# Attention scores as three fp16 passes instead of one fp32 pass, with a mask, a low half and weight pieces put elsewhere

## The chip, the core and the metric

One NeuronCore of a Trainium2 chip runs the program. It has a matrix engine (TensorE, PE in the profile; its weight loads are listed as PEld), VectorE (DVE), ScalarE (ACT), GpSimd (POOL) and SyncE (SP), which issues most DMAs. Each engine works through its own queue in the order in which the program was written, and waits in place when what it needs isn't there. The metric is the device time of one execution in microseconds; the time of a kernel is the median of its runs.

## What is computed

Keys and values of 8 batches, 8 heads and 576 rows are averaged over 8 rows each, so that 72 pooled keys remain. The attention over them gives 4608 rows of 512, and each row then goes through one of 8 experts (a matrix of 512x1024, a ReLU, a matrix of 1024x512), chosen by the largest of 8 logits, and is scaled by the softmax of that logit.

```python
k_p = k.reshape(B, H, Sp, pool, D).mean(axis=3)
v_p = v.reshape(B, H, Sp, pool, D).mean(axis=3)
scores = scale * np.matmul(q, k_p.transpose(0, 1, 3, 2))
attn = np.exp(scores - np.max(scores, axis=-1, keepdims=True))
attn = attn / (np.sum(attn, axis=-1, keepdims=True) + 1e-09)
out = np.matmul(attn, v_p)
...
h = np.maximum(x_sorted[lo:hi] @ w1[e], 0.0)
y_sorted[lo:hi] = h @ w2[e]
```

## The kernel before

The program has two parts. The attention takes the first 190 us, in 36 **units** (a unit is 128 query rows of one batch with all 8 heads; every ninth unit takes 64 rows of each of two batches). The experts take the rest, in blocks of 256 rows, and were left alone.

The order is written by hand: the loop at line 975 emits unit after unit, and `put(i, position, f)` hangs a step on a position of unit i (`q`, `pe`, `act`, `dve`, `pe2`, `sp`, `act2`, `dve2`), which `run(i, position)` emits there. What concerns the change, in the order of one unit i:

- `u_pt` (line 487) turns unit i's probabilities P with five transposes into the PSUM tile `pp`, which has one buffer, and ScalarE copies them to `pt` (line 496). In seven units one more matmul puts the mask `mk` beside them in `pp` (line 494).
- `g_s` (line 452) makes the scores of two heads (a half stage A here, a half stage Z at the unit's end), by one fp32 matmul a head. Such a matmul serves two units: on its 128 partitions stand the 64 features of a query row of one unit and the 64 of a row of the other, and the keys stand twice in `BD` (three tiles, one a batch), in the upper 64 partitions for the first 72 columns and in the lower 64 for the other 72, with zeros beside them. So 144 columns come out. The turned queries stand in `qT`.
- `g_qt` (line 432) turns four heads of a later group of queries into a PSUM tile `pq`, and ScalarE copies it to `qT` (line 445).
- `k_pe`, `v_pe` and `u_pe` each come once a batch, in units of their own: they turn the pooled keys, turn the pooled values, and multiply the values by the router's matrix. Each writes a `pq` tile. `k_act` and `v_act` (lines 362, 379) copy the keys from it into the first half of `BD`; for batches 2 to 7 a DMA collected in `moves` (line 1012) then copies them into the second half.
- `g_min` (line 477) takes the smallest score on VectorE, `g_exp` (line 484) the exponentials on ScalarE.
- `masked` (line 410) writes the masked values V into `VB`, on VectorE, from the mask in `pp`.
- `u_pv` (line 498) multiplies `pt` by V into `po`, which has one buffer; `u_nrm` (line 531) divides by the sums on VectorE (lines 544, 546, 548) and so frees `po`. Between its steps `fill()` emits steps of the router of an earlier group (lines 588 to 658).

All of `g_qt`, `k_pe`, `v_pe`, `u_pe` and the router share the tile name `pq` with **two buffers, used in turn**: whoever comes next takes the buffer used the time before last, and must wait until its readers are done. `wsplit` (line 104) splits an expert's weights into fp16 halves; its pieces `h` and `s` are ScalarE work over 128x1024 each, at `act` and `act2` of units 12 to 31 in the table at line 832.

## Time and profile before

| | |
|---|---|
| median of 3 runs | 605.59 us (604.68 to 605.96) |
| the profiled execution | 608.13 us, span of its instructions 606.2 us |
| busy share of the span | PE 96%, PEld 72%, DVE 44%, ACT 47%, POOL 45% |
| granted TensorE clock, mean | 0.99 |

The span is counted from the first instruction; all positions in the trace are microseconds from there. A busy matmul is counted from its issue to its modelled end, so two that overlap fill the row without a gap; the PEld rows show better when TensorE takes up the next piece of work. In brackets stands how long an engine sat idle ahead of an instruction, and what released it.

### The profile page before, as it was taken

The page shows a single profiled execution, that of the slowest core. Times are in us where ns is not written, and L with a number is a line of the kernel's source. Part 1 is how long each engine was busy: PE and PEld are TensorE (multiplying, and loading weights), DVE is VectorE, ACT ScalarE, POOL GpSimd, SP SyncE. Part 2 cuts the span into 40 slices and gives each one's busy share as a digit, 9 for nine tenths or more (in the row PEclk, how much of TensorE's full clock was granted, in tenths as well). Part 3 has the DMA queues.
Part 4 walks back from the last instruction along what each step waited for, and adds up shares of the span by engine and source line. Part 5 has one row for each costly group of instructions (what it writes and reads, how often), then busy time and mean ns, then how long its engine had stood idle before and what let it go on. Part 6 is the DMA issues. An engine that isn't in the chain of part 4 may idle for free.

```text
span 606.2 us, 15226 instructions
## 1 busy us (share of the span) xinstructions
PE 581.4 (96%) x4473; PEld 436.6 (72%) x4474; DVE 268.2 (44%) x545; ACT 285.0 (47%) x633; POOL 270.7 (45%) x527
## 2 busy tenths in 40 slices
PE   7899999999998989989999999999999999999995
PEld 7788999999894747747676765767756677567663
DVE  6545655675664264025752873323623471133022
ACT  2766688889931262226642762233522452222122
POOL 5798899997966424220432332122411242211212
PEclk9999999999999999998999999999999999999999
DMA  8999899784594549942987689143332224421200
GB/s 250 302 313 242 293 319 283 266 278 155 142 312 166 175 120 326 341 101 63 311 260 222 181 263 341 61 108 82 79 91 52 83 62 108 108 49 39 69 17 32
DMA packets 96271, 107.10 MB, mean 177 GB/s; under 512 B 54446, under 2 KB 64686, under 8 KB 96240
## 3 DMA queue, kind: packets, MB, share of 16 engines
q1 hardware_dynamic: 89520, 85.42, 49.6%
q0 software_dynamic: 6720, 21.28, 9.3%
q8 instruction: 17, 0.28, 0.2%
q14 instruction: 14, 0.11, 0.1%
HBM read 72.99 MB, written 23.37 MB: 159 GB/s over the span
## 4 chain that ended last, share of the span: by engine, by line
PE 51%; PEld 4%; issue 3%; ACT 1%; PEldq 0%; POOLq 0%; ACTq 0%; DVE 0%; POOL 0%; DVEq 0%
PE po L1042 14%; PE pq L1042 11%; PE ps L964 6%; PE pp L964 3%; PE pq L964 3%; PE ps L955 2%; PE ps L956 2%; PE ps L957 2%; PEld L964 1%; PEld L1042 1%; PE pp L957 1%; PE pq L956 1%; PE pq L957 1%; PE pp L955 1%; PE pq L955 1%
## 5 line engine op out<-in xcount | busy, mean ns | idle before, releaser
L1042 PEld LDWEIGHTS <-bd 128*128 128x128 f16 x936 | 91.3, 98 | 110.1 <-issue 3.1
L1203 POOL TENSOR_TENSOR spacer<-ql,iG 1x1 f32<-1x1 f32 x44 | 20.8, 472 | 199.2 <-ACT ql L1199 191.8
L1036 DVE SCALAR_TENSOR_TENSOR bd<-ps,bd 128x512 f16<-128x512 f32 (+1 forms) x44 | 27.6, 630 | 182.8 <-ACT bd L1033 180.0
L484 ACT ACTIVATE both<-ps,nmx 128x72 f32<-128x72 f32 x288 | 68.9, 349 | 3.1 <-DVE nmx L477 3.1
L1033 ACT ACTIVATE bd<-ps 128x512 f16<-128x512 f32 (+1 forms) x44 | 24.1, 549 | 96.4 <-PE L964 76.3
L513 PE MATMUL po<-vb,pt 128*128 128x146 f32 (+5 forms) x480 | 66.8, 301 | 1.2 <-ACT pt L496 1.2
L513 PEld LDWEIGHTS po<-vb,pt 128*128 128x128 f32 (+1 forms) x480 | 62.1, 178 | 4.4 <-ACT pt L496 2.5
L1042 PE MATMUL po<-w,bd 128*128 128x512 f16 x264 | 59.3, 379 | 1.0 <-issue 1.0
L1042 PE MATMUL po<-kv,bd 128*128 128x512 f16 x264 | 58.8, 379 | 0.0
L964 PEld LDWEIGHTS <-qt 128*128 128x128 f16 x528 | 48.6, 99 | 11.8 <-issue 4.7
L1204 POOL DMA_INDIRECT out_dram<-ql,iG x44 | 46.2, 1051 | 21.0 <-issue 19.9
L964 PEld LDWEIGHTS <-w 128*128 128x128 f16 x480 | 42.1, 100 | 10.8 <-ACT kv L114 2.8
L1042 PE MATMUL pq<-kv,bd 128*128 128x512 f16 x216 | 48.1, 379 | 0.0
L467 PE MATMUL ps<-bd,qT 128*128 128x144 f32 x256 | 44.4, 297 | 2.5 <-DVE bd L739 0.8
L1042 PE MATMUL pq<-w,bd 128*128 128x512 f16 x192 | 44.7, 389 | 1.6 <-ACT bd L1033 1.6
L1199 ACT ACTIVATE ql<-po,gB 128x512 f32<-128x512 f32 x22 | 15.0, 683 | 57.7 <-PE L964 36.2
L663 POOL DMA_INDIRECT x_by_expert<-both,rpos x36 | 35.5, 987 | 13.1 <-issue 5.6
L467 PEld LDWEIGHTS ps<-bd,qT 128*128 128x128 f32 x256 | 34.9, 190 | 3.6 <-DVE bd L739 0.9
L477 DVE TENSOR_REDUCE nmx<-ps 128x4 f32<-128x288 f32 x72 | 32.0, 452 | 11.1 <-PE ps L467 10.3
L496 ACT ACTIVATE pt<-pp 128x640 f32<-128x640 f32 x36 | 25.5, 709 | 23.3 <-PE pp L491 14.3
L964 PE MATMUL ps<-kv,qt 128*128 128x256 f16 (+1 forms) x264 | 32.8, 266 | 3.6 <-issue 2.7
L864 DVE TENSOR_TENSOR bd<-vb,bd 128x1024 f16<-128x1024 f32 x22 | 27.0, 1225 | 19.1 <-ACT bd L861 9.2
(243 smaller groups left out, 1194.8 us busy)
## 6 DMA issues: line engine op xcount, KB each, us to landing
both<-in_moe_w_dram SPq DMA_DIRECT2D x6, 2048.0 KB, 12.2
st<-in_moe_w_dram SPq DMA_DIRECT2D x6, 2048.0 KB, 13.7
vb<-x_by_expert SPq DMA_DIRECT2D x16, 578.0 KB
st<-in_moe_w_dram SPq DMA_DIRECT2D x8, 1024.0 KB
kv<-in_k_dram SPq DMA_DIRECT2D x6, 1024.0 KB
kv<-in_v_dram SPq DMA_DIRECT2D x6, 1024.0 KB
qt<-in_q_dram SPq DMA_DIRECT2D x6, 1024.0 KB
kv<-in_k_dram SPq DMA_DIRECT2D x4, 512.0 KB
```

The costliest lines, as they stand in the source:

```text
L467: nc.tensor.matmul(ps[:, x * 2 * KP:(x + 1) * 2 * KP], t[:, h, :], BD[b % 3][:, :, h, :], start=True, stop=True)
L477: nc.vector.tensor_reduce(nmx, ps[:, 0:4 * KP].rearrange("p (h x) -> p h x", x=KP), axis=AX.X, op=OP.min)
L484: nc.scalar.activation(p[:, h * KP:(h + 1) * KP], ps[:, x * KP:(x + 1) * KP], AF.Exp, bias=nmx[:, x:x + 1], scale=-1.0)
L496: nc.scalar.activation(pt, pp[:, 0:640], AF.Copy)
L513: nc.tensor.matmul(po[m, half, cols], pt[:, c * 128 + m.start:c * 128 + m.stop], VB[(b + s) % 3][:, c, sl, 0:CW], start=first.get(half, Tr ...
L663: st = nc.gpsimd.indirect_dma_start(out=xs, out_offset=bass.IndirectOffsetOnAxis(ap=Z["pos"][:, u:u + 1], axis=0), in_=X[:, u, :], in_offs ...
L864: nc.vector.tensor_tensor(col(xh[:, :, 1]), row(xg), col(xh[:, :, 0]), op=OP.subtract)
L955: nc.tensor.matmul(dst, wh, xT[:, d, 0:n], start=(d == 0), stop=False)
L964: nc.tensor.matmul(dst, W1[s][z][:, d, c], xT[:, x, 0:n], start=(z == 0 and x == 0), stop=(z == 1 and d == DC - 1))
L1036: V.scalar_tensor_tensor(pair(hT[1], k, n), ups_of(k, n), 0.0, pair(hT[0], k, n), op0=OP.max, op1=OP.subtract)
L1042: nc.tensor.matmul(y, hT[x][:, f, 128 * j:128 * j + 128], W2[s][z][:, f, :], start=(half == x == z == f == 0), stop=(half == z == 1 and f ...
L1204: st = nc.gpsimd.indirect_dma_start(out=out, out_offset=bass.IndirectOffsetOnAxis(ap=iG[:, j:j + 1], axis=0), in_=ys[j], in_offset=None, b ...
```

## The change

The scores no longer use fp32 operands. Queries and keys are each held as a high fp16 number and a low fp16 number (the rest), and `g_s` adds three passes, high by high, low by high and high by low, in one accumulation. The queries are scaled by 2^-3 and the keys by its inverse. `BD` and `qT` become fp16 tiles with one more index for high and low; they keep their size.

The high halves are written by the ScalarE copies that were there. The low halves are new VectorE instructions that read the same PSUM tile `pq` again: `q_low`, of 128x512, behind `g_min(A)` of the unit; and `k_low`, of 64x512 for the keys that `k_pe` turned and 64x64 for those that `v_pe` did, collected in `klows` and emitted by `k_lows` at the unit's end, behind `act2` and `dve2`. The copy into the second half of `BD` (`moves`) goes out there too, for both halves of the number in one DMA, and no longer ahead of `g_s(Z)`. At the start batch 0 gets the same: its second half moves from VectorE (line 739) to ScalarE, and two `k_low` and a `q_low` follow on VectorE.

Two further steps move. `masked` has a position of its own, `mask`, ahead of `g_min(A)`. The `h` and `s` pieces of the weights move mostly from the end of a unit to the new position `pt` of the next, straight behind ScalarE's copy of the turned P.

```diff
-    BD = [loads.tile([128, 2, H, KP], F32, name=f"bd{i}") for i in range(3)]
+    BD = [loads.tile([128, 2, 2, H, KP], F16, name=f"bd{i}") for i in range(3)]
...
-    SC = 1.0 / (POOL * math.sqrt(D))
+    SC = 1.0 / (POOL * math.sqrt(D) * SQ)
...
+    def k_low(b, s, src, lo, hi):
+        nc.vector.scalar_tensor_tensor(half(b, s, 1)[:, lo:hi], src, -SC, half(b, s, 0)[:, lo:hi], op0=OP.mult,
+                                       op1=OP.subtract)
+
+    klows = []
+
+    def k_lows():
+        while klows:
+            k_low(*klows.pop(0))
+        while moves:
+            nc.sync.dma_start(*moves.pop(0))
...
-            nc.scalar.activation(half(b, s)[:, 0:512], pm[64 * s:64 * s + 64, :], AF.Copy, scale=-SC)
+            nc.scalar.activation(half(b, s, 0)[:, 0:512], pm[64 * s:64 * s + 64, :], AF.Copy, scale=-SC)
+            klows.append((b, s, pm[64 * s:64 * s + 64, :], 0, 512))
...
-            moves.append((half(b, 1), half(b, 0)))
+            moves.append((BD[b % 3][64:128, :, 1], BD[b % 3][0:64, :, 0]))
...
-            QT[G] = work.tile([128, 8, 128], F32, name="qT", bufs=2)
+            QT[G] = work.tile([128, 2, 8, 128], F16, name="qT", bufs=2)
...
-            nc.scalar.activation(QT[G][:, 4 * j:4 * j + 4, :].rearrange("p h t -> p (h t)"), pq, AF.Copy)
+            nc.scalar.activation(qh, pq, AF.Copy, scale=SQ)
+            return lambda: nc.vector.scalar_tensor_tensor(qw, pq, SQ, qh, op0=OP.mult, op1=OP.subtract)
...
+    PASS = ((0, 0), (1, 0), (0, 1))
...
-                nc.tensor.matmul(ps[:, x * 2 * KP:(x + 1) * 2 * KP], t[:, h, :],
-                                 BD[b % 3][:, :, h, :], start=True, stop=True)
+                for y, z in PASS:
+                    nc.tensor.matmul(ps[:, x * 2 * KP:(x + 1) * 2 * KP], t[:, y, h, :], BD[b % 3][:, z, :, h, :],
+                                     start=(y, z) == PASS[0], stop=(y, z) == PASS[-1])
...
-    nc.vector.tensor_scalar(half(0, 1), pm[64:128, 0:H * KP], -SC, None, op0=OP.mult)
+    nc.scalar.activation(half(0, 1, 0), pm[64:128, 0:H * KP], AF.Copy, scale=-SC)
+    q_low()
+    for s in range(2):
+        k_low(0, s, pm[64 * s:64 * s + 64, 0:H * KP], 0, H * KP)
...
-        put(at, "dve", masked, b)
+        put(at, "mask", masked, b)
...
-    for j, h, x, p in ((0, (12, "act2"), (13, "act2"), 15), (1, (14, "act2"), (17, "act2"), 24),
+    for j, h, x, p in ((0, (13, "pt"), (14, "pt"), 15), (1, (15, "pt"), (18, "pt"), 24),
...
         run(i, "pe")
+        run(i, "mask")
         if A:
             g_min(*A)
+        for f in lows:
+            f()
+        if A:
             fill()
...
-        while moves:
-            nc.sync.dma_start(*moves.pop(0))
         if Z:
             g_s(*Z)
         u_nrm(i, (lambda: g_min(*Z)) if Z else None)
         run(i, "act2")
         run(i, "dve2")
+        k_lows()
```

Three places show what stands in a row. The first is VectorE in unit 24, which turns the keys of batch 7 and also begins the router of units 18 to 23 (L588 to L612 before, L609 to L633 in the change). Before, from the two minima (L477) to the next two:

```order
L477 TENSOR_REDUCE nmx<-ps 128x4 x2
L588 TENSOR_REDUCE pq<-both 128x48
L590 TENSOR_REDUCE rm<-pq 128x6
L594 TENSOR_TENSOR ra<-pq,rm 128x48
L595 TENSOR_TENSOR pq<-pq,rm 128x48
L544 TENSOR_SCALAR ri<-po 128x8
L601 TENSOR_TENSOR pq<-pq,down 128x48
L602 TENSOR_REDUCE rm_1976<-pq 128x6
L546 RECIPROCAL ri<-ri 128x8
L612 TENSOR_TENSOR roh<-pq,rm_1976 128x48
L548 TENSOR_TENSOR both<-po,ri 128x576
```

In the change the same stretch begins so (L462 is `q_low`):

```order
L498 TENSOR_REDUCE nmx<-ps 128x4 x2
L462 SCALAR_TENSOR_TENSOR qT<-pq,qT 128x512
L609 TENSOR_REDUCE pq<-both 128x48
L611 TENSOR_REDUCE rm<-pq 128x6
L615 TENSOR_TENSOR ra<-pq,rm 128x48
```

and ends so (L352 is `k_low`, L569 the last step of `u_nrm`):

```order
L622 TENSOR_TENSOR pq<-pq,down 128x48
L623 TENSOR_REDUCE rm_2269<-pq 128x6
L567 RECIPROCAL ri<-ri 128x8
L633 TENSOR_TENSOR roh<-pq,rm_2269 128x48
L569 TENSOR_TENSOR both<-po,ri 128x576
L498 TENSOR_REDUCE nmx<-ps 128x4
L352 SCALAR_TENSOR_TENSOR bd_155<-pq,bd_155 64x512
```

`q_low` now stands ahead of the router's steps and of `u_nrm`, and `k_low` behind `u_nrm` and the minimum of Z.

The second place is TensorE in unit 25, from the scores of A to the turned values, before (with what an instruction waits for in brackets; L440 turns the queries, L368 the values):

```order
L467 MATMUL ps_1996<-bd0_154,qT_1887 128x144 [waits DVE_49,Activation_49]
L467 MATMUL ps_1996<-bd0_154,qT_1887 128x144
L440 MATMUL pq_2003<-ident_67,qt0_150 128x128 [waits Activation_49]
L440 MATMUL pq_2003<-ident_67,qt0_150 128x128 x3
L368 MATMUL pq_2010<-ident_67,vp_1800 128x128 [waits DVE_49,Pool_49]
```

and in the change (L488, L455 and L382 are the same steps):

```order
L488 MATMUL ps_2290<-bd0_154,qT_2162 128x144
L488 LDWEIGHTS qT_2162
L488 MATMUL ps_2290<-bd0_154,qT_2162 128x144
L455 MATMUL pq_2301<-ident_67,qt0_150 128x128 [waits DVE_49,PE_49]
L455 MATMUL pq_2301<-ident_67,qt0_150 128x128 x3
L382 MATMUL pq_2308<-ident_67,vp_2057 128x128 [waits DVE_49,PE_49,Pool_49]
```

The turn of the queries takes the buffer that `k_pe` of unit 24 used. It waited for ScalarE's copy of the keys, and now waits for VectorE, whose last reading of that buffer is `k_low`.

The third place is ScalarE around unit 24 (L496 and L517 copy the turned P, L445 and L461 the queries, L118 and L119 are an `s` piece). Before:

```order
L118 ACTIVATE st_64<-st_64 128x1024
L496 ACTIVATE pt<-pp 128x640
L445 ACTIVATE qT<-pq 128x512
L484 ACTIVATE both<-ps,nmx 128x72 x8
L362 ACTIVATE bd_155<-pq 64x512
L598 ACTIVATE rex<-ra 128x48
```

and in the change:

```order
L517 ACTIVATE pt<-pp 128x640
L119 ACTIVATE st_64<-st_64 128x1024
L461 ACTIVATE qT<-pq 128x512
L505 ACTIVATE both<-ps,nmx 128x72 x8
L375 ACTIVATE bd_155<-pq 64x512
L619 ACTIVATE rex<-ra 128x48
```

The piece has gone from ahead of the copy of P to between it and the copy of the queries.

## Rows read from the trace of the kernel before

**Rows 1.** Busy time by stretch: start:end, length, engines, granted clock, DMA share, GB/s.

```profile
33.00:139.00 106.00, 105.54 (x877) 100.20 (x878) 61.74 (x179) 85.04 (x283) 97.70 (x105) 1.00 0.90 281
139.00:169.00 30.00, 28.81 (x244) 26.94 (x243) 17.74 (x55) 27.69 (x81) 25.12 (x41) 1.00 0.57 169
190.00:204.00 14.00, 11.20 (x51) 4.85 (x51) 4.91 (x31) 2.46 (x4) 3.92 (x11) 0.88 0.30 98
```

**Rows 2.** Timeline of weight loads, units 24 and 25: start, length, engine, line, count.

```profile
133.48 0.55 PEld L467 LDWEIGHTS ps<-bd,qT 128*128 128x128 f32 x4
133.96 0.59 PEld L491 LDWEIGHTS pp<-ident,both 128*128 128x128 f32 x5
...
135.00 0.48 PEld L440 LDWEIGHTS pq<-ident,qt 128*128 128x128 f32 x4
...
136.15 1.76 PEld L513 LDWEIGHTS po<-vb,pt 128*128 128x128 f32 x12
...
139.57 0.48 PEld L440 LDWEIGHTS pq<-ident,qt 128*128 128x128 f32 x4
```

**Rows 3.** Timeline of TensorE: fp16 matmuls of 128 (L722) and 256 columns.

```profile
11.18 0.61 PE L722 MATMUL po<-ones 128*128 128x128 f16 x8
...
168.49 0.27 PE L955 MATMUL ps<-kv,w 128*128 128x256 f16 x1
...
168.70 0.27 PE L957 MATMUL ps<-kv,w 128*128 128x256 f16 x1
```

**Rows 4.** Groups by line and shape: busy us, mean ns of one, idle before.

```profile
L1036 DVE SCALAR_TENSOR_TENSOR bd<-ps,bd 128x512 f16<-128x512 f32 x34 | 23.4, 691 | 135.0 <-ACT bd L1033 132.1 <-issue 2.8
...
L118 ACT ACTIVATE st<-st 128x1024 f32<-128x1024 f32 x8 | 9.0, 1126 | 0.0
```

**Rows 5.** Timeline of VectorE, units 24 and 25.

```profile
132.29 0.86 DVE L588 TENSOR_REDUCE pq<-both 128x48 f32<-128x384 f32 x1 [0.54 <-ACT qT L445]
...
134.44 0.75 DVE L548 TENSOR_TENSOR both<-po,ri 128x576 f32<-128x576 f32 x1
135.10 0.81 DVE L477 TENSOR_REDUCE nmx<-ps 128x4 f32<-128x288 f32 x2
...
139.58 0.20 DVE L635 TENSOR_TENSOR rt<-pq,roh 128x48 f32<-128x48 f32 x1
```

**Rows 6.** Timeline of ScalarE, unit 24.

```profile
130.74 0.71 ACT L496 ACTIVATE pt<-pp 128x640 f32<-128x640 f32 x1 [0.31 <-PE pp L491]
131.66 0.60 ACT L445 ACTIVATE qT<-pq 128x512 f32<-128x512 f32 x1 [0.22 <-PE pq L440]
```

**Rows 7.** Timeline of VectorE and weight loads, units 6 and 7.

```profile
57.66 0.91 DVE L477 TENSOR_REDUCE nmx<-ps 128x4 f32<-128x288 f32 x2
...
57.78 0.49 PEld L440 LDWEIGHTS pq<-ident,qt 128*128 128x128 f32 x4
```

**Rows 8.** The same two engines, units 15 and 16.

```profile
96.40 0.92 DVE L477 TENSOR_REDUCE nmx<-ps 128x4 f32<-128x288 f32 x2
...
96.99 0.25 PEld L368 LDWEIGHTS pq<-ident,vp 128*128 128x128 f32 x2
```

**Rows 9.** The same two engines, units 19 and 20.

```profile
113.64 0.20 DVE L635 TENSOR_TENSOR rt<-pq,roh 128x48 f32<-128x48 f32 x1
...
113.80 0.48 PEld L440 LDWEIGHTS pq<-ident,qt 128*128 128x128 f32 x4
```

**Rows 10.** The same two engines, unit 18 and the start of unit 19's `u_pv`.

```profile
106.67 0.87 DVE L588 TENSOR_REDUCE pq<-both 128x48 f32<-128x384 f32 x1 [1.11 <-ACT qT L445]
...
110.15 1.77 PEld L513 LDWEIGHTS po<-vb,pt 128*128 128x128 f32 x12
```

**Rows 11.** Timeline of VectorE, GpSimd and weight loads, start of the program.

```profile
11.74 0.76 DVE L739 TENSOR_SCALAR bd<-pp 64x576 f32<-64x576 f32 x1 [1.86 <-ACT bd L738]
...
18.42 0.19 POOL L773 TENSOR_TENSOR spacer<-vp 1x1 f32<-1x1 f32 x1 [9.33 <-DVE vp L335]
...
32.21 0.11 PEld L370 LDWEIGHTS pq<-ident,vp 128*64 128x64 f32 x1 [1.31 <-POOL vp L314]
```

More of the change, by code (lines that the diff above doesn't have):

```diff
@@ L25 @@
 UPAT = (33, 34, 35)
+SQ = 2.0 ** -3
 HS = (0, 1, 3, 5, 5)
@@ L345, in pool_v, with half @@
         pool(kv[(2 * b + 1) % 3], KVS["vp", b], (part,))
-    def half(b, s):
-        return BD[b % 3][64 * s:64 * s + 64, s].rearrange("p h x -> p (h x)")
+    def half(b, s, y):
+        return BD[b % 3][64 * s:64 * s + 64, y, s].rearrange("p h x -> p (h x)")
+    def k_low(b, s, src, lo, hi):
[7 more added lines that the diff above has]
+            nc.sync.dma_start(*moves.pop(0))
     def k_pe(b):
@@ L378, in v_act @@
         for s in range(min(b, 2) and 3 - min(b, 2)):
-            nc.scalar.activation(half(b, s)[:, 512:576], pm[64 * s:64 * s + 64, 384:448], AF.Copy, scale=-SC)
+            nc.scalar.activation(half(b, s, 0)[:, 512:576], pm[64 * s:64 * s + 64, 384:448], AF.Copy, scale=-SC)
+            klows.append((b, s, pm[64 * s:64 * s + 64, 384:448], 512, 576))
         if b > 1:
-            moves.append((half(b, 1), half(b, 0)))
+            moves.append((BD[b % 3][64:128, :, 1], BD[b % 3][0:64, :, 0]))
         vT = KVS["vT", b] = work.tile([128, 384], F32, name="vT", bufs=1)
@@ L441, in g_qt @@
         if j == 0:
-            QT[G] = work.tile([128, 8, 128], F32, name="qT", bufs=2)
+            QT[G] = work.tile([128, 2, 8, 128], F16, name="qT", bufs=2)
+        qh, qw = (QT[G][:, y, 4 * j:4 * j + 4, :].rearrange("p h t -> p (h t)") for y in range(2))
         def put_q():
-            nc.scalar.activation(QT[G][:, 4 * j:4 * j + 4, :].rearrange("p h t -> p (h t)"), pq, AF.Copy)
+            nc.scalar.activation(qh, pq, AF.Copy, scale=SQ)
+            return lambda: nc.vector.scalar_tensor_tensor(qw, pq, SQ, qh, op0=OP.mult, op1=OP.subtract)
         return put_q if hold else put_q()
@@ L458, in g_s @@
                 for s in range(2):
-                    bd = BD[(b + s) % 3].rearrange("p s h x -> p (s h) x")
-                    rhs = bd[:, 2 * x:2 * x + H + 2:H + 1, :]
-                    nc.tensor.matmul(ps[64 * s:64 * s + 64, (x % 2) * 2 * KP:(x % 2 + 1) * 2 * KP],
-                                     t[:, x, 64 * s:64 * s + 64], rhs, start=True, stop=True)
+                    for y, z in PASS:
+                        rhs = BD[(b + s) % 3][:, z].rearrange("p s h x -> p (s h) x")[:, 2 * x:2 * x + H + 2:H + 1, :]
+                        nc.tensor.matmul(ps[64 * s:64 * s + 64, (x % 2) * 2 * KP:(x % 2 + 1) * 2 * KP],
+                                         t[:, y, x, 64 * s:64 * s + 64], rhs, start=(y, z) == PASS[0],
+                                         stop=(y, z) == PASS[-1])
             slots = [(4 * j + x, 0) for x in range(4)]
@@ L466, in g_s @@
             for x, h in enumerate(hs):
-                nc.tensor.matmul(ps[:, x * 2 * KP:(x + 1) * 2 * KP], t[:, h, :],
-                                 BD[b % 3][:, :, h, :], start=True, stop=True)
+                for y, z in PASS:
+                    nc.tensor.matmul(ps[:, x * 2 * KP:(x + 1) * 2 * KP], t[:, y, h, :], BD[b % 3][:, z, :, h, :],
+                                     start=(y, z) == PASS[0], stop=(y, z) == PASS[-1])
             slots = [(h, s) for h in hs for s in range(2)]
@@ L735 @@
     turned((4, 2, 3))
-    g_qt(0, 0)
+    q_low = g_qt(0, 0)
     turned((0, 1))
-    nc.scalar.activation(half(0, 0), pm[0:64, 0:H * KP], AF.Copy, scale=-SC)
-    nc.vector.tensor_scalar(half(0, 1), pm[64:128, 0:H * KP], -SC, None, op0=OP.mult)
-    g_qt(0, 1)
+    nc.scalar.activation(half(0, 0, 0), pm[0:64, 0:H * KP], AF.Copy, scale=-SC)
+    nc.scalar.activation(half(0, 1, 0), pm[64:128, 0:H * KP], AF.Copy, scale=-SC)
+    q_low()
+    for s in range(2):
+        k_low(0, s, pm[64 * s:64 * s + 64, 0:H * KP], 0, H * KP)
+    q_low = g_qt(0, 1)
     nc.tensor.matmul(warm[:, 0, 384:399], ident, mk.rearrange("p c s -> p (c s)"), start=True, stop=True)
@@ L746 @@
     g_min(0, 1)
+    q_low()
     g_exp(0, 1)
@@ L755 @@
     keep_warm(8)
-    turned_q()
+    turned_q()()
     u_pt(0)
@@ L760 @@
     v_act(0)
-    g_qt(1, 1)
+    q_low = g_qt(1, 1)
     now(1, 0)
@@ L767 @@
     g_min(1, 1)
+    q_low()
     load_qh(1, 0)
@@ L981 @@
             u_pt(i)
+        run(i, "pt")
+        lows = []
         if i == 0:
-            g_qt(*turns.pop(i))
+            lows.append(g_qt(*turns.pop(i)))
         if A:
@@ L989 @@
         if i in turns:
-            g_qt(*turns[i])
+            lows.append(g_qt(*turns[i]))
         if Y and keyed:
```

2 lines of the change are left out of this document (1 added, 1 removed), and 6 rows, old and new, of the table n.

## The prediction

> **What bounds the kernel now.** I read first the busy time by stretch [rows 1], because the change touches only the attention, and its share has three phases. Between 33 and 139 us TensorE is busy 105.5 of 106 us with its clock at 1.00; VectorE has 44 us to spare there and ScalarE 21. Between 139 and 169 us ScalarE is the fullest beside TensorE, 27.7 of 30 us. So what shortens TensorE's rows before 139 us shortens the program, unless TensorE is made to wait; after it that is no longer sure.
>
> The timeline of weight loads then gives the price of each piece, since one piece begins where the last ends [rows 2]: a half stage of scores is two fp32 matmuls, and from its first load to that of the next piece pass 133.96 - 133.48 = 0.48 us. In this stretch TensorE goes from piece to piece with hardly an idle bracket. That is the thing to look for: the order of before has just enough distance between a piece and what it waits for, and a new wait on a `pq` buffer costs its whole length.
>
> **The passes.** The trace of before has no 144-column fp16 matmul. Its nearest are 256 columns, each with a weight load of its own, which start 0.105 us apart (168.49 to 168.70 for two), and 128 columns: eight in 0.61 us, and since a single one of 256 shows 0.27 - 0.105 = 0.165 us of tail, (0.61 - 0.165)/8 = 0.056 us apart [rows 3]. On the line between these, 144 columns make 0.062 us. Six of them make 0.375 us in place of 0.48: **0.105 us saved** for a half stage. By the ends 0.056 and 0.105 us it would be +0.14 saved or 0.15 lost. I take 0.062, because 144 lies next to 128. Units 2 to 26 with one batch hold 44 such half stages in the stretch that TensorE bounds: 44 x 0.105 = **-4.6 us** (ends -6.4 and +6.6). The half stages of units with two batches are 64 rows each and I count nothing for them; the 14 after 139 us lie under ScalarE.
>
> The Trainium skill ("TensorE: Matmul & The Clock Gate", section "Back-to-back issue gap") says that a stream of weight load and matmul pairs holds about 81 ns a matmul at 128 columns, where 56 ns is the gap of a lone one. The eight of [rows 3], which load weights each, speak against it at 56 ns. By the page six passes would be an estimated 0.5 us, and the saving gone. It is the third rival below.
>
> **The low halves on VectorE.** Nothing like them stands in the attention of before, but the experts have the same operation, out of PSUM with an fp16 operand, 128x512 in 0.69 us [rows 4]; I take 0.65 to 0.69 for `q_low` and for the 64x512 `k_low` (fewer partitions don't shorten an instruction: 64x576 took 0.76 us [rows 11]). At 256 columns the same line would be cheaper, so the lower bound is half, 0.35 us; the upper is the 0.76 of the start. Some 26 `q_low` in the stretch are 18 us of VectorE's 44 spare ones. Throughput is therefore no issue; what matters is who stands behind them, and when the buffer comes free.
>
> **Unit 24 to 25, the worst place.** In the change `g_qt` of unit 25 waits for `k_low` of unit 24, which stands behind `q_low`, the router's start, `u_nrm` and two minima. P's copy starts at 130.74 and `qT` at 131.66 [rows 6]. An `s` piece of 1.05 us (its row, 1.13, is modelled with overlap [rows 4]) is now between them: `qT` comes at 132.4 and is done at 133.0. `q_low` takes VectorE to 133.65, where the router started at 132.29 [rows 5]: 1.36 later. From there VectorE is a chain without a gap, so the minima of Z go from 135.10 to 136.46; the later of the two ends 0.4 after that for the first and `k_low` runs from about 136.86 to 137.55. TensorE wants `g_qt` at 135.00 [rows 2], less three saved half stages, 134.7. Hold: **2.85 us**. Half as long a low step would leave 2.2.
>
> **The other units with `k_low`.** The same reading at the other four, always from the last instruction of VectorE and the load that wants the buffer: unit 6 to 7, minima at 57.66 begin 0.55 later for `q_low` and `k_low` ends at 59.3, wanted at 57.78 less three half stages: 1.8 [rows 7]. Unit 15 to 16, without a router's start: the first minimum at 96.40 ends and `k_low` runs to about 97.4, for a `pq` wanted at 96.7: 0.7 [rows 8]; it stands ahead of the values' turn at 96.99. Unit 19 to 20: behind a router step at 113.64, `k_low` to 114.5 for 113.80 less three: 0.8 [rows 9]. Unit 10 to 11 is like 15 to 16 with less before it: 0.55. Sum with unit 24: **+6.7 us**. Where `v_pe`'s buffer has a 64x64 `k_low` (short, but again behind `u_nrm` and the minima) I get 0.7 at units 7 to 8 and 25 to 26 and 0.25 at 11 to 12 and 20 to 21: **+1.9 us**. All of them are bounded below by nought (if VectorE is ahead, nobody waits) and above by one and a half times.
>
> **Routers without keys.** In unit 18 the router begins at 106.67, behind `qT` [rows 10]; a weight piece ahead of the copy makes `qT` 1.0 later, `q_low` adds 0.65, and the last of `u_nrm`, which frees `po`, ends at 111.25 instead of 109.6 (where the minima of Z begin). `u_pv` wanted it at 110.15 [rows 10], less two half stages, 109.9: 1.4. In unit 12 it is 0.5 in the same way. **+1.9 us.**
>
> **The start.** VectorE copied the second half of batch 0's keys in 0.76 us at 11.74 [rows 11]; that copy goes to ScalarE, ahead of the first scores either way, and `q_low` and two `k_low` (some 2 us) come on VectorE, ahead of the pooling of V that GpSimd waits for (row at 18.42). Values' turns later wait 1.31 us for GpSimd (row at 32.21) [rows 11], so this delay reaches TensorE. Part of it lies in waits that are there: **+1.0 us**, from 0 to 2.
>
> **Costed at nothing.** The mask of V moves ahead of `g_min(A)`: 1.1 us of VectorE in seven units, which delays the minima and the exponentials by as much, but ScalarE has 21 us spare in the stretch and the turned P of the next unit is not the last to come; without that cover up to 1 us each. The `moves` go out some 2 us later on SP; what they copy is needed three units on, and behind them on SP's queue stand loads that are as far from their use. The weight pieces move by half a unit, in both directions, and ScalarE's total over 139 to 169 us stays at 27.7 of 30 [rows 1]: 0, between -0.7 and +1.5.
>
> **Sum.** -4.6 + 6.7 + 1.9 + 1.9 + 1.0 = +6.9 us. The profiled execution took 608.13 us, 2.5 over the median of the runs (605.59) and spread over all of it, so by itself it would become 615.0; against the median, **612.5 us**.
>
> **Rivals.** First, the holds don't bite: VectorE gets to `k_low` before TensorE comes, because TensorE itself has been slowed by something else or the short form of the low step is cheap. For it: VectorE is idle 42% of the stretch. Against it: in unit 24 its rows stand end to end. The passes' saving and half of the start's delay remain, 605.59 - 4.6 + 0.5 = 601.5 us. Second, half of the holds: 605.59 - 4.6 + 1.0 + 5.25 = 607.2, or 606.4 with the low step at half its length in the K units; I take 606.4, no change. Third, the passes save nothing (the skill's rule, above): 612.5 + 4.6 = 617.1. The eight at 56 ns speak against it; for it only that they share one operand and these don't. Fourth, the hold at unit 25 lets the clock fall from 2.4 to 1.2 GHz for a time. In 190 to 204 us, where TensorE stands idle for 2.8 of 14 us, it was granted 0.88 on the mean of the two levels [rows 1]; a hold of 2.85 us that costs a like share of the 14 us after it is 0.12 x 14 = 1.7 us, 614.2. The rival that ends on the other side is the first; it decides where `k_low` of unit 24 ends ahead of 134.7 us, and for that the router would have to start ahead of the copy of the queries and the low steps to take a third of their price.
>
> **Chances.** Forecast 0.56 (its own range 608.5 to 616), first rival 0.19, second 0.13, third 0.06, fourth 0.06. A measurement of this kernel can tell 0.2% from no change, that is 604.4 to 606.8 us. Faster by more: all of the first rival and a little of the second, 0.20. Within: most of the second, 0.10. Slower: 0.70. The range reaches from within the first rival's upper end, 603.5 us (its time with 2 us of the holds left), to the third, 617.5.
>
> **What would show it.** The weight loads of a half stage should take 0.37 us and not 0.48. The load of `g_qt` in units 7 and 25 should carry an idle bracket of about 1.8 and 2.9 us, released by VectorE's `k_low`; if the bracket is missing the first rival holds. Unit 18's `router` rows should begin some 1.6 us later against the copy of P, and `u_pv` of unit 19 wait for `po`. From 33 to 139 us the stretch should grow by about 6 us, and after 169 us nothing should change. I am wrong if the half stage costs 0.48 or over, if the holds are found elsewhere (the mask's units 3, 10, 15, 20, 22), or if the stretch of ScalarE absorbs them.

## The result, and the profile after

The changed kernel took 614.36 us (median of 4 runs, 613.73 to 617.62) against 605.78 us of before in the same comparison (604.68 to 608.21): a ratio of 1.0147, 95% interval 1.0100 to 1.0194. Forecast were 612.5 us and a range of 603.5 to 617.5. The profiled execution of the change took 614.17 us with a span of 612.4; the forecast for it was 615.0. Runs that are slow as a whole, at a lower mean clock, are left out of the ratios, and the traces of two experiments (weight pieces back, one pass) are of such runs.

The busy time by stretch, with the columns of [rows 1]; the stretches are moved to where the same units now run (units 2 to 25, 27 to 33, and the opening of the experts):

```profile
36.00:146.50 110.50, 102.80 (x994) 93.95 (x994) 81.06 (x217) 85.10 (x283) 96.20 (x105) 1.00 0.84 262
146.50:178.00 31.50, 28.16 (x268) 25.50 (x266) 20.60 (x61) 27.44 (x80) 24.64 (x42) 0.95 0.59 167
200.00:214.00 14.00, 10.30 (x56) 4.79 (x54) 4.89 (x31) 2.46 (x4) 3.19 (x9) 1.00 0.35 110
```

TensorE was busy 105.5 of 106 us in its full stretch; it is now idle for 7.7 of 110.5. VectorE went from 61.7 to 81.1 us and is still far from full. So the loss is not throughput but waiting, as the forecast had it. Where it comes in is read from the start of the copy of P of each unit (the rows `pt<-pp` of ScalarE):

| copy of P of unit | before, us | change, us | later by |
|---|---|---|---|
| 0 | 18.68 | 19.96 | 1.28 |
| 2 | 34.21 | 37.22 | 3.01 |
| 7 | 57.58 | 59.30 | 1.72 |
| 12 | 79.28 | 82.31 | 3.03 |
| 18 | 104.59 | 108.21 | 3.62 |
| 20 | 113.59 | 118.29 | 4.70 |
| 26 | 139.46 | 146.56 | 7.10 |
| 30 | 156.73 | 163.36 | 6.63 |
| 32 | 164.65 | 174.22 | 9.57 |
| 35 | 175.75 | 185.19 | 9.44 |

At the attention's end the change is 9.4 us behind, and by the span's end 6.2: in these two executions the experts took 3.2 us less (below).

Up to unit 2 the delay has two steps. From the first turn of the queries (9.89 us before, 9.56 in the change) to unit 0's copy of P pass 8.79 us before and 10.40 in the change. From there to unit 2's copy pass 15.53 and 17.26. In both steps TensorE waits for `k_low` itself, because the scores need the low half of the keys (those of batch 0 at 13.59 and of batch 1 at 31.24; the weight loads of unit 1's `u_pv` follow):

```profile
13.59 0.79 PE L488 MATMUL ps<-bd,qT 128*128 128x144 f16 x10 [1.27 <-DVE bd L352]
...
31.24 0.41 PE L488 MATMUL ps<-bd,qT 128*128 128x144 f16 x4 [1.20 <-DVE bd L352]
...
32.05 3.20 PEld L534 LDWEIGHTS po<-vb,pt 128*128 128x128 f32 x12
```

The matmuls and their waits, from the groups by line and shape (the columns of [rows 4]; L488 are the scores, L455 the turn of the queries, L382 of the values, L352 is `k_low`, L633 the router, L418 the step that puts the router's products into `VB`, L462 `q_low`):

```profile
L462 DVE SCALAR_TENSOR_TENSOR qT<-pq,qT 128x512 f16<-128x512 f32 x36 | 24.8, 688 | 29.0 <-ACT qT L461 27.9 <-ACT both L505 1.1
L352 DVE SCALAR_TENSOR_TENSOR bd<-pq,bd 64x512 f16<-64x512 f32 x8 | 5.4, 676 | 1.6 <-ACT bd L375 1.6
L455 PE MATMUL pq<-ident,qt 128*128 128x128 f32 x128 | 20.3, 283 | 4.0 <-DVE vb L418 1.2 <-DVE roh L633 1.0 <-DVE bd L352 0.8
L382 PE MATMUL pq<-ident,vp 128*128 128x128 f32 x16 | 3.2, 283 | 3.1 <-DVE bd L352 3.1
L488 PE MATMUL ps<-bd,qT 128*128 128x144 f16 x384 | 35.7, 230 | 5.4 <-DVE bd L352 2.5 <-ACT both L505 1.4 <-ACT bd L375 0.6
```

The low steps cost 0.69 and 0.68 us each, the price of [rows 4]. The idle time ahead of the turns of queries and values, 7.1 us together, is what the forecast called holds. Of it 3.9 us are released by `k_low` (L352); the rest by `q_low` or VectorE steps that stand behind it. The 2.5 us ahead of the scores are the two waits just shown.

The place that the forecast called the worst, unit 24 to 25: VectorE and ScalarE first (the columns of [rows 5, 6]), then TensorE's two turns.

```profile
136.57 1.05 ACT L119 ACTIVATE st<-st 128x1024 f32<-128x1024 f32 x1
137.51 0.59 ACT L461 ACTIVATE qT<-pq 128x512 f16<-128x512 f32 x1
...
138.13 0.69 DVE L462 SCALAR_TENSOR_TENSOR qT<-pq,qT 128x512 f16<-128x512 f32 x1 [1.04 <-ACT qT L461]
138.86 0.87 DVE L609 TENSOR_REDUCE pq<-both 128x48 f32<-128x384 f32 x1
...
140.86 0.21 DVE L633 TENSOR_TENSOR roh<-pq,rm 128x48 f16<-128x48 f32 x1
...
142.02 0.67 DVE L352 SCALAR_TENSOR_TENSOR bd<-pq,bd 64x512 f16<-64x512 f32 x1
...
141.22 0.63 PE L455 MATMUL pq<-ident,qt 128*128 128x128 f32 x4 [0.76 <-DVE roh L633]
142.83 0.41 PE L382 MATMUL pq<-ident,vp 128*128 128x128 f32 x2 [0.99 <-DVE bd L352]
```

The piece, the copy of the queries, `q_low`, the router and `k_low` come in the forecast order, each at the end of the one before. But two tiles wait, not one: the turn of the queries waits for the router's last step, which used the other buffer, and the turn of the values for `k_low`. In unit 6 to 7 the same pair shows 0.22 and 0.99 us.

What a half stage costs is seen in the weight loads. Two of them, at the ends of units 7 and 9, each followed by the turn of P (L512):

```profile
63.95 0.37 PEld L488 LDWEIGHTS <-qT 128*128 128x128 f16 x6
64.29 0.53 PEld L512 LDWEIGHTS pp<-ident,both 128*128 128x128 f32 x5
...
72.21 0.46 PEld L488 LDWEIGHTS <-qT 128*128 128x128 f16 x6
72.63 0.53 PEld L512 LDWEIGHTS pp<-ident,both 128*128 128x128 f32 x5
```

0.34 us in one and 0.42 in the other; over the rows of units 2 to 25 it is 17.07 us for 249 matmuls, 0.069 us each, so 0.41 us for six where two fp32 ones took 0.48. In these rows, from load to load without the brackets, TensorE needs 5.6 us less than before (100.6 to 95.0), and its brackets grow by 9.7 us (4.1 to 13.8): the stretch gets 4.1 us longer.

### The profile page after: what moved, and what is told of

Read it like the earlier page. It is cut to its first block, busy times and chain, and to the rows that moved or that the text cites. A ratio compares the mean times of both kernels' runs of the same rounds, so it can differ in the third digit from the quotient of the medians.

```text
span 612.4 us, 15519 instructions
## 1 busy us (share of the span) xinstructions
PE 575.9 (94%) x4633; PEld 428.4 (70%) x4634; DVE 297.1 (49%) x598; ACT 285.8 (47%) x634; POOL 271.4 (44%) x527
## 4 chain that ended last, share of the span: by engine, by line
PE 58%; DMA 2%; issue 2%; ACT 2%; DVE 1%; POOL 1%; ACTq 0%; POOLq 0%; SPq 0%; PEld 0%; PEldq 0%; DVEq 0%
PE po L1073 15%; PE pq L1073 13%; PE ps L990 7%; PE pq L990 4%; PE pp L990 4%; PE ps L983 3%; PE ps L982 3%; PE ps L981 3%; PE pp L981 1%; PE pp L983 1%; PE pp L982 1%; PE pq L981 1%; PE pq L982 1%; PE pq L983 1%; DMA kv<-bd 1%
## 5 line engine op out<-in xcount | busy, mean ns | idle before, releaser
L534 PE MATMUL po<-vb,pt 128*128 128x146 f32 (+5 forms) x480 | 68.6, 306 | 3.3 <-DVE both L569 1.8
L534 PEld LDWEIGHTS po<-vb,pt 128*128 128x128 f32 (+1 forms) x480 | 63.6, 182 | 7.8 <-ACT pt L517 4.5
L1073 PE MATMUL pq<-w,bd 128*128 128x512 f16 x192 | 43.3, 379 | 0.5 <-ACT bd L1064 0.4
L488 PE MATMUL ps<-bd,qT 128*128 128x144 f16 x384 | 35.7, 230 | 5.4 <-DVE bd L352 2.5
L462 DVE SCALAR_TENSOR_TENSOR qT<-pq,qT 128x512 f16<-128x512 f32 x36 | 24.8, 688 | 29.0 <-ACT qT L461 27.9
L517 ACT ACTIVATE pt<-pp 128x640 f32<-128x640 f32 x36 | 25.5, 707 | 24.5 <-PE pp L512 15.9
L320 POOL TENSOR_TENSOR st<-kv 128x1280 f32<-128x1280 f32 x12 | 34.9, 2905 | 0.1
```

The lines of the kernel that those rows point to most:

```text
L320: nc.gpsimd.tensor_tensor(t1, src[:, :, 0:4 * D], src[:, :, 4 * D:], op=OP.add)
L488: nc.tensor.matmul(ps[:, x * 2 * KP:(x + 1) * 2 * KP], t[:, y, h, :], BD[b % 3][:, z, :, h, :], start=(y, z) == PASS[0], stop=(y, z) == PA ...
L534: nc.tensor.matmul(po[m, half, cols], pt[:, c * 128 + m.start:c * 128 + m.stop], VB[(b + s) % 3][:, c, sl, 0:CW], start=first.get(half, Tr ...
L1073: nc.tensor.matmul(y, hT[x][:, f, 128 * j:128 * j + 128], W2[s][z][:, f, :], start=(half == x == z == f == 0), stop=(half == z == 1 and f ...
```

## The experiments

Three groups of four kernels ran on a chip each, and before ran beside each group; its medians there were 607.12, 600.60 and 606.55 us. So the ratio to before is what is compared, with its 95% interval; the change, which ran only in the first comparison, has 1.0147 (1.0100 to 1.0194). The ratios are those on record, and differ by up to 0.3% from the quotients of the medians.

### No low half of K

```diff
-        while klows:
-            k_low(*klows.pop(0))
+        klows.clear()
```

> The changed kernel without the low half of K from batch 1 on: the k_low instructions behind the unit's end are left out and that half stays zero; passes, q_low and all places stay as they are. Theory (v_pe waits for k_low as the last reader of its PSUM buffer): the brackets at the values' turn in units 7, 11, 16 and 25 (1.20, 0.81, 0.48, 1.20 us) and the hold of unit 1 (1.32) go, some 4 to 5 us in all, so 609.5 to 611 us where the change took 614.4 and before 605.8; the wait of g_qt in unit 25 for the router (0.92) stays. Rival (TensorE would wait there for GpSimd's pooled values or for something else anyway): 613.5 to 614.5 and the brackets stay with another releaser.

608.96 us, ratio 1.0026 (1.0004 to 1.0049). `k_low` from batch 1 on is thus worth 1.2% or some 7 us, more than the 4 to 5 expected. At the attention's end the run is 2.2 us behind before instead of 9.4. In unit 25 the values' turn waits only 0.29 us, now for the router, and the wait of the queries' turn, which was expected to stay, is gone:

```profile
134.51 0.64 PE L454 MATMUL pq<-ident,qt 128*128 128x128 f32 x4
135.44 0.41 PE L381 MATMUL pq<-ident,vp 128*128 128x128 f32 x2 [0.29 <-DVE roh L632]
```

Nobody waits for GpSimd there, so that rival is out.

### No low halves, three high passes

```diff
-            return lambda: nc.vector.scalar_tensor_tensor(qw, pq, SQ, qh, op0=OP.mult, op1=OP.subtract)
+            return lambda: None
...
-    PASS = ((0, 0), (1, 0), (0, 1))
+    PASS = ((0, 0), (0, 0), (0, 0))
```

`k_low` is out as well, this time with the two of batch 0 at the start, and each pass starts its sum anew.

> The changed kernel without any low half: neither k_low nor q_low is issued, and each half stage runs the high by high pass three times, so TensorE's instructions are as many and as long as in the change. Theory (passes save about 0.07 to 0.1 us a half stage, and all of the loss is waits behind VectorE): 600 to 603 us, faster than before at 605.8. Rival (the passes save nothing, or the moved mask and pieces cost by themselves): 605.5 to 608.

603.44 us, ratio 0.9932 (0.9909 to 0.9955): 4.1 us under before, with all steps of the change at their new places. So the passes do save, the moved steps cost nothing that shows, and the three parts of the bill are -4.1 us for the passes, some 5.7 for `q_low` and the start's two `k_low` together (1.0026 - 0.9932), and some 7.3 for the other `k_low` (1.0147 - 1.0026), each ratio times 606. By the intervals of the ratios these parts are uncertain by an estimated 1.4, 1.9 and 3.2 us. `q_low` was never left out alone, so the split holds for this order of leaving out.

### Weight pieces back

```diff
-    for j, h, x, p in ((0, (13, "pt"), (14, "pt"), 15), (1, (15, "pt"), (18, "pt"), 24),
+    for j, h, x, p in ((0, (12, "act2"), (13, "act2"), 15), (1, (14, "act2"), (17, "act2"), 24),
...
```

> The changed kernel with only the weight pieces at their old positions in the table. Theory (a piece between the copy of P and the copy of the queries delays qT by 1.05 us, and through q_low the router, in units 18 and 24): 1.5 to 2.5 us less than the change, 612 to 613. Rival (the pieces are covered, ScalarE has room): within 0.5 us of 614.4. A third: they are worth something to ScalarE's stretch behind 146 us, and putting them back costs 0.5 to 1.5 us more.

613.74 us, ratio 1.0094 (1.0061 to 1.0126). The interval overlaps that of the change, so by the time alone it is open. In its trace the attention ends 1.6 us earlier than in the change, and unit 24's `q_low` waits less for the copy of the queries:

```profile
136.99 0.69 DVE L462 SCALAR_TENSOR_TENSOR qT<-pq,qT 128x512 f16<-128x512 f32 x1 [0.61 <-ACT qT L461]
```

1.04 us of idle VectorE became 0.61. That agrees with the theory's direction and size, but the trace's span is 619.3 us, longer than the change's by 7, so the mechanism is likely and not shown.

### The mask back

```diff
-        put(at, "mask", masked, b)
+        put(at, "dve", masked, b)
```

> The changed kernel with only the masked values back behind the exponentials, at their old position. Theory (the mask's 1.13 us on VectorE ahead of the minima is covered): within 0.7 us of the change at 614.4. Rival (in its seven units it delays the minima, q_low and what stands behind them): 612 to 613.

621.44 us, ratio 1.0226 (1.0193 to 1.0260): worse than the change by some 5 us, which neither theory had. Unit 22 to 23 shows why (L425 writes V from the mask in `pp`, L512 turns the next P into `pp`):

```profile
131.65 0.69 DVE L462 SCALAR_TENSOR_TENSOR qT<-pq,qT 128x512 f16<-128x512 f32 x1 [1.69 <-ACT qT L461]
...
132.32 1.13 DVE L425 TENSOR_TENSOR vb<-vp,pp 128x960 f32<-128x960 f32 x1
133.38 0.15 DVE L565 TENSOR_SCALAR ri<-po 128x8 f32<-128x8 f32 x1
...
133.60 0.74 PE L512 MATMUL pp<-ident,both 128*128 128x128 f32 x5 [1.88 <-DVE ri L565]
```

`pp` has one buffer, and the masked V is its last reader. Behind `q_low`, which waits 1.69 us for ScalarE, it holds `pp` until 133.45, and the next turn of P waits 1.88 us. (Its row names the short L565 behind the mask; but it starts 0.15 us after L425 ends, as the values' turn of unit 25 starts 0.14 after `k_low`.) At its new place it runs while VectorE waits for the queries. The move pays for nothing of its own; it keeps `q_low` from costing still more.

### More idle matmuls at the start

```diff
-    keep_warm(8)
+    keep_warm(32)
     now(0, 0)
```

> The changed kernel with 32 instead of 8 idle matmuls of 128 columns ahead of the first scores, where TensorE sat idle from 12.2 to 13.6 us and the clock was granted 0.62 and 0.52 in the two stretches behind it (14 to 18 us). Theory (the idle time lets the clock fall, and the fall costs 1 to 1.5 us at the start): the clock stays at 1.00 up to 18 us and the time is 0.8 to 1.5 us under the change's 614.4. Rival (TensorE waits for VectorE and ScalarE there, so a slower clock costs nothing): clock 1.00, time within 0.5 us of the change. Second rival (the clock falls for another reason): clock as low as before.

611.68 us, ratio 1.0179 (1.0144 to 1.0213): no gain over the change. The clock was up this time; the two rows of the change first, then of this run:

```profile
10.00:14.00 4.00, 2.10 (x27) 1.85 (x26) 2.20 (x3) 2.37 (x4) 0.36 (x2) 1.00 1.08 275
14.00:18.00 4.00, 3.47 (x35) 3.20 (x33) 3.86 (x8) 1.95 (x9) 0.00 (x0) 0.57 0.79 266
```

```profile
10.00:14.00 4.00, 3.27 (x54) 3.15 (x53) 2.57 (x4) 2.16 (x4) 0.35 (x2) 1.00 1.14 291
14.00:18.00 4.00, 2.88 (x38) 2.29 (x35) 3.90 (x9) 2.36 (x11) 0.00 (x0) 1.00 1.02 329
```

VectorE is busy 3.9 of the 4 us in both: it sets the pace there, and a faster TensorE only waits longer (3.47 us busy became 2.88). From the first turn of the queries to the first copy of P pass 10.46 us, 10.40 in the change. The first rival holds. That the idle matmuls kept the clock up isn't shown: the run with `k_low` behind `q_low` (below) has 8 of them and 1.00 from 14 to 18 us too, and also 10.46 us.

### Keys' halves made from SBUF

```diff
+            if b > 1:
+                kc = KVS["kc"] = work.tile([64, 576], F32, name="kc", bufs=1)
+                nc.scalar.activation(kc[:, 0:512], pm[0:64, :], AF.Copy, scale=-SC)
+                continue
...
+            nc.vector.tensor_copy(half(b, 0, 0), kc)
+            nc.vector.tensor_tensor(half(b, 0, 1), kc, half(b, 0, 0), op=OP.subtract)
```

> The changed kernel, where for batches 2 to 7 ScalarE copies the turned keys as fp32 into an SBUF tile and VectorE makes both halves from that at the end of the v_pe unit (two instructions more than nothing, 64x576 each). VectorE works as much as in the change or more, but the PSUM buffer is free as soon as ScalarE has read it. Theory (the hold is the buffer, not VectorE's load): the values' turn in units 7, 11, 16, 25 doesn't wait for VectorE, 3 to 4.5 us under the change, 610 to 611.5. Rival (VectorE's time is what is short): within 1 us of 614.4 or above.

607.82 us beside 600.60 of before, ratio 1.0129 (1.0088 to 1.0170), level with the change. The values' turns of units 7, 11 and 16 wait no more for VectorE, as the theory had it, but a new hold of 3.1 us came up, once, in unit 6:

```profile
51.30 3.33 DVE L355 TENSOR_TENSOR bd<-kc,bd 64x576 f16<-64x576 f32 x1
...
50.91 3.11 POOL L320 TENSOR_TENSOR st<-kv 128x1280 f32<-128x1280 f32 x1
...
57.26 0.38 PEld L501 LDWEIGHTS <-qT 128*128 128x128 f16 x6 [3.14 <-ACT pt L530]
57.28 0.54 PE L501 MATMUL ps<-bd,qT 128*128 128x144 f16 x6 [2.93 <-DMA bd<-bd]
```

A subtraction of 64x576 took 3.33 us and ended behind a GpSimd step that had begun before it; the next took 1.30 and the other four 0.75. The copy of the keys' second half goes out behind it, and by TensorE's own row the scores wait for that. So neither theory alone: the buffer was a hold, and VectorE on two SBUF operands is a new one.

### The router's scratch in SBUF

```diff
-            pm = psA.tile([128, 512], F32, name="pq", bufs=2)
-            for n, x in enumerate(("L", "eq", "eqd")):
-                Z[x] = pm[:, 64 * n:64 * n + gs * E].rearrange("p (u e) -> p u e", e=E)
+            pm = work.tile([128, 48], F32, name="rsb", bufs=1)
+            for x in ("L", "eq", "eqd"):
+                Z[x] = pm[:, 0:gs * E].rearrange("p (u e) -> p u e", e=E)
```

> The changed kernel with the router's scratch (logits and the two masks of the best) in SBUF instead of one of the two PSUM buffers. Theory (g_qt waits for the router's last reading of its buffer in units 7, 20 and 25: 0.38, 0.46 and 0.92 us, and the router starts 0.7 to 1.4 us later for q_low): the buffers shift by one, g_qt no longer waits for the router, but the values' turn still waits for k_low: 0.5 to 2 us under the change, 612.5 to 614. Rival (k_low's buffer now comes to g_qt, which wants it earlier than the values' turn did): 0 to 2 us above the change.

626.43 us, ratio 1.0426 (1.0391 to 1.0461), far outside both expectations. Unit 12 to 13:

```profile
90.23 2.84 DVE L633 TENSOR_TENSOR roh<-rsb,rm 128x48 f16<-128x48 f32 x1
...
90.12 2.88 POOL L320 TENSOR_TENSOR st<-kv 128x1280 f32<-128x1280 f32 x1
...
93.88 2.47 PE L534 MATMUL po<-vb,pt 128*128 128x146 f32 x8 [3.25 <-DVE both L569]
```

The same comparison of 128x48 takes 0.21 us in the change, where one operand lies in PSUM, and there in the midst of the same addition of GpSimd:

```profile
87.24 0.21 DVE L633 TENSOR_TENSOR roh<-pq,rm 128x48 f16<-128x48 f32 x1
...
87.04 2.90 POOL L320 TENSOR_TENSOR st<-kv 128x1280 f32<-128x1280 f32 x1
```

With both in SBUF it ends only when GpSimd's addition, begun 0.11 us earlier, does. Other steps of the router are stretched in the same way (1.50, 2.27, 2.19 and 1.14 us among them, some 9.5 us in all over their times in the change), and behind the waits that follow, four `u_pv` have loads of 2.98 to 3.37 us instead of 1.76. The Trainium skill (SBUF — State Buffer, "SBUF: two separate sides") has this rule: VectorE with two SBUF inputs and a GpSimd step that reads SBUF exclude each other for a whole instruction; both traces agree, this one with 2.84 us and the one above with 3.33.

### Those three together

The keys from SBUF, the router's scratch in SBUF and 32 idle matmuls, each as above.

> The last three together: keys' halves from SBUF, the router's scratch in SBUF, 32 idle matmuls at the start. Theory (buffers held by VectorE are what costs): 605 to 608, level with before (605.8), since 2.8 us under before were left with no low half at all. Rival (VectorE's load is what costs): 610 or above.

627.23 us, ratio 1.0421 (1.0377 to 1.0465): the rival's side, but by its rows for the reason just shown and not for VectorE's load: steps of the router took 2.00 and 2.82 us there, the keys' first subtraction 3.33.

### `k_low` right behind `q_low`

```diff
+        for x in [x for x in hooks.get((i, "act"), []) if x[0] is k_act]:
+            hooks[i, "act"].remove(x)
+            x[0](*x[1])
         if A:
             g_min(*A)
         for f in lows:
             f()
+        k_lows()
```

> The changed kernel with ScalarE's copy of the turned keys ahead of the exponentials of A and k_low right behind q_low, so that it reads the PSUM buffer before u_nrm and the minima of Z. Theory (the hold at the values' turn is the distance of k_low from its copy): the 1.20, 0.81, 0.48 and 1.20 us at units 7, 11, 16 and 25 go, against 0.6 us more ahead of the router in units 6 and 24: 1.5 to 3 us under the change (ratio to before 1.010 to 1.0125 where the change has 1.0147). Rival (the queue of VectorE only passes the delay on, to the router and po): ratio 1.014 to 1.018.

613.69 us, ratio 1.0095 (1.0064 to 1.0126). That is under the expected window, though its interval overlaps that of the change; the attention ends 2.8 us earlier than there (6.6 us behind before). Of these, 1.3 us are there by unit 2, where `k_low` has its old wait in unit 1 but the clock didn't fall behind it:

```profile
31.61 0.41 PE L488 MATMUL ps<-bd,qT 128*128 128x144 f16 x4 [1.20 <-DVE bd L352]
...
32.18 1.77 PEld L534 LDWEIGHTS po<-vb,pt 128*128 128x128 f32 x12
```

In unit 25 the values' turn still waits, but for another:

```profile
137.12 0.68 DVE L352 SCALAR_TENSOR_TENSOR bd<-pq,bd 64x512 f16<-64x512 f32 x1 [0.60 <-ACT bd L375]
...
140.06 0.41 PE L382 MATMUL pq<-ident,vp 128*128 128x128 f32 x2 [1.12 <-DVE roh L633]
```

So by the rows both sides hold a part: the waits of the values' turns in units 11 and 16, where no router stands, are gone (0.60 and 0.28 us in the change), and in the router's units the queue passes the delay on.

### One pass

```diff
-    PASS = ((0, 0), (1, 0), (0, 1))
+    PASS = ((0, 0),)
```

Both low halves are out, those of the start too, as in the run with three high passes.

> The changed kernel with the high by high pass alone: no low halves and two of three passes left out, to see what a pass is worth. Theory (TensorE bounds units 2 to 26, a pass of a half stage is 2 x 0.069 us): two passes less take 0.27 us from each half stage, 8 to 12 us in all by TensorE alone, cut short where GpSimd (97.7 of 106 us busy there) or ScalarE is next: 4 to 8 us under the run with three high passes, that is a ratio to before of 0.980 to 0.987. Rival (TensorE isn't the bound any more without the waits): ratio 0.990 to 0.994, as with three passes.

606.62 us, ratio 0.9980 (0.9946 to 1.0015): against the theory and even against the rival, two passes less gave nothing over the run with three. The trace shows what TensorE then waits for:

```profile
43.86 0.44 PE L381 MATMUL pq<-ident,vp 128*128 128x128 f32 x2 [1.98 <-POOL vp L323]
...
54.88 0.40 PE L487 MATMUL ps<-bd,qT 128*128 128x144 f16 x2 [3.48 <-DMA bd<-bd]
...
115.79 0.69 PE L381 MATMUL pq<-ident,vp 128*128 128x128 f32 x2 [2.93 <-POOL vp L323]
...
56.58 3.41 PEld L533 LDWEIGHTS po<-vb,pt 128*128 128x128 f32 x12
```

GpSimd's pooled values, and once the DMA of the keys' second half, come later than TensorE. Behind such a wait the 12 loads of `u_pv` take 3.41 us and not 1.76: the clock has fallen. GpSimd was busy 97.7 of 106 us before [rows 1], so nothing under it can be gained from the scores. That `u_pv` at 1.2 GHz is what takes the rest away fits the rows but wasn't tried by itself.

### The mask alone, and the pieces alone, in the kernel before

```diff
+        run(i, "mask")
         if A:
             g_min(*A)
...
-        put(at, "dve", masked, b)
+        put(at, "mask", masked, b)
```

> The kernel before with only the masked values at the new position, directly behind the mask. Theory (the mask is read from the one buffer of the turned P; where nothing long stands ahead of it on VectorE its place is worth little): ratio 0.997 to 1.002. Rival (the moved mask helps by itself, since the buffer comes free earlier): 0.993 to 0.997. Other rival (it delays the minima and the exponentials): above 1.002.

607.38 us, ratio 1.0015 (0.9985 to 1.0044): no difference, as the theory had it.

```diff
+        run(i, "pt")
...
-    for j, h, x, p in ((0, (12, "act2"), (13, "act2"), 15), (1, (14, "act2"), (17, "act2"), 24),
+    for j, h, x, p in ((0, (13, "pt"), (14, "pt"), 15), (1, (15, "pt"), (18, "pt"), 24),
...
```

> The kernel before with only the weight pieces at their new positions. Theory (a piece ahead of the copy of the queries makes that copy 1.05 us later, and the router of units 18 and 24 with it): 0.5 to 2 us over before, ratio 1.001 to 1.003. Rival (covered): 0.999 to 1.001. Other rival (the places are better for ScalarE): under 0.999.

608.44 us, ratio 1.0004 (0.9974 to 1.0035): no difference that can be told. In its trace the attention ends 2.8 us later than before; but in the trace of the mask alone, where no piece moves, it ends 1.7 us later, so two single executions differ by nearly as much anyway. Whether the pieces cost something that the rest covers stays open.

No version with all its low halves beats before.

## Why the prediction was right, and where not

**The passes.** Forecast 0.375 us a half stage and -4.6 us; measured 0.41 us, and -4.1 us by the run without low halves. In the rows of units 2 to 25 the spans between loads shrink by 5.6 us, of which only 2.6 in the scores (19.65 to 17.07 us) and the rest in the pieces beside them, mostly the turns of P (13.35 to 12.07) and of the queries (10.82 to 9.98). The forecast had the scores alone. So the term is right in size, but the saving for a half stage was taken too large and that of the neighbours left out. At 0.057 to 0.070 us for 144 columns with a weight load each, the rate that the third rival drew from the Trainium skill (TensorE: Matmul & The Clock Gate, "Back-to-back issue gap"), 81 ns at 128 columns, isn't seen here.

**The holds of `k_low`.** Forecast 6.7 + 1.9 = 8.6 us; leaving `k_low` out gave some 7.3. The mechanism is right: `k_low` frees the buffer late, and TensorE waits. But the places and sizes are not those of the forecast. On PE's rows in the change:

| unit that waits | forecast, us | waits for `k_low` | waits for the router |
|---|---|---|---|
| 7 | 1.8 | 0.99 | 0.22 |
| 11 | 0.55 | 0.60 | |
| 16 | 0.7 | 0.28 | |
| 20 | 0.8 | none | 0.30 |
| 25 | 2.85 | 0.99 | 0.76 |
| 8 and 26, 64x64 | 0.7 each | 0.39 each | |
| 12 and 21, 64x64 | 0.25 each | none | |
| 4 | not in it | 0.29 | |

That is 3.9 us of 8.6. In units 7, 20 and 25 the forecast let `g_qt` wait for `k_low`; there `g_qt` waits for the router, whose scratch takes a buffer between them, and in 7 and 25 the values' turn `v_pe` waits for `k_low` (for unit 16 the forecast had the values' turn). The 7.3 us also hold what the forecast didn't have: the scores of unit 1, which wait for the low keys themselves and not for a buffer, with the fall of the clock behind them. From unit 0's copy of P to unit 2's pass 17.26 us in the change and 15.24 without `k_low`, 2.0 us. So it is partly luck that 8.6 lies near 7.3.

**`q_low`.** This is the most mis-sized term. I gave it 1.9 us in the routers of units 12 and 18 and 1.0 at the start, 2.9 in all; leaving it out as well, with the start's two `k_low`, gave some 5.7 us. At the start it was not the way over GpSimd that I gave: TensorE waits for the low halves directly, and the way to unit 0's copy of P is 1.6 us longer (10.50 us without the later `k_low`, 8.30 without any low half, 8.79 before). In unit 18 the router began 3.74 us behind the copy of P instead of 2.08, 1.66 later, as forecast; but `u_pv` of unit 19 didn't wait for `po`. Ahead of it `g_qt` had waited 0.87 us for a `pq` buffer, which L418 on VectorE frees late. And I had the stretch bound by ScalarE at nought with an end at +1.5: the delay there grows from 7.1 to 9.4 us. In the router's unit 30 `q_low` stands ahead of the router, and the next `u_pv` waits 1.77 us for `po`, where before it waited 0.16 for `pt` (last row):

```profile
166.42 0.69 DVE L462 SCALAR_TENSOR_TENSOR qT<-pq,qT 128x512 f16<-128x512 f32 x1 [1.19 <-ACT qT L461]
167.03 0.86 DVE L609 TENSOR_REDUCE pq<-both 128x48 f32<-128x384 f32 x1
...
169.15 0.74 DVE L569 TENSOR_TENSOR both<-po,ri 128x576 f32<-128x576 f32 x1
170.04 1.21 PE L534 MATMUL po<-vb,pt 128*128 128x146 f32 x7 [1.77 <-DVE both L569]
```

```profile
161.34 1.76 PEld L513 LDWEIGHTS po<-vb,pt 128*128 128x128 f32 x12 [0.16 <-ACT pt L496]
```

Without `k_low` the same wait is 1.78 us, so it is `q_low`'s; without any low half it is 0.97, and for ScalarE. It is the mechanism that the forecast worked out for units 12 and 18, and it should have been worked out for 30 too.

**The experts.** Forecast: nothing changes after 169 us. In the two profiled executions they took 3.2 us less in the change. Before, the second expert waited 2.81 us for its weights, and its loads took 5.51 us behind that, the granted clock being 0.72 from 225 to 231 us; in the change the wait is 2.04 us, with no fall. Last the kernel before with the pieces moved:

```profile
225.16 5.51 PEld L964 LDWEIGHTS <-w 128*128 128x128 f16 x36 [2.81 <-ACT kv L114]
```

```profile
233.94 3.84 PEld L990 LDWEIGHTS <-w 128*128 128x128 f16 x36 [2.04 <-ACT kv L115]
```

```profile
228.27 3.84 PEld L964 LDWEIGHTS <-w 128*128 128x128 f16 x36 [2.86 <-ACT kv L114]
```

The waits differ by 0.77 us and the loads by 1.67, so 2.4 of the 3.2 us are seen here. That they are the change's doing isn't shown: the pieces alone waited 2.86 us without a fall, the mask alone 2.99 us with one, and from the last copy of P to the end these two took 428.8 and 427.5 us, before 430.4 and the change 427.2. The profiled execution of before was itself 2.5 us over its median; by the medians the change loses 8.6 us, so most of the 9.4 stays.

**The fourth rival**, the clock, came in as a part and not at unit 25, where the granted clock stayed at 1.00. It fell at 32 to 35 us (0.50) behind the waits of unit 1, where 12 loads of `u_pv` took 3.20 us instead of 1.76, and after 170 us (0.69 to 174) behind the 1.77 us of `u_pv`. The same waits in unit 1 stand in seven other traces with `k_low`: in two of them the loads took 3.32 and 2.92 us, in five 1.77. So the fall doesn't come each time, and the medians hold it as often as it came.

**What was costed at nothing** held for mask and pieces, which alone make no difference in before that can be told. But the mask's place isn't free in the change: its old one would have cost some 5 us.

In sum: -4.1 + 7.3 + 5.7 = 8.9 us against a forecast of +6.9 and a measured 8.6. The direction and the mechanism, waits behind VectorE that cost more than the passes save, were forecast and are shown. That the total came so near is luck in part. By the copies of P the start cost 3.0 us instead of 1.0, units 2 to 25 cost 4.1 instead of 5.9 (8.6 + 1.9 - 4.6), ScalarE's stretch 2.3 instead of 0, and the misses partly cancel.
